# K's transform as 64 by 32 points in 32x64 tiles, the second table's magnitudes by 512 small exponentials, and a new order

## The chip, the cores and the metric

One core of one Trainium2 chip. TensorE (PE) multiplies matrices; its weight loads are a row of their own in the profile (PEld). VectorE (DVE) and ScalarE (ACT) do elementwise work, ScalarE also the exponentials, sines and sigmoids. SyncE (SP) issues every DMA. The metric is device microseconds of the core, as the median of several runs; the profile is one execution, and its span begins at its first and ends at its last record.

## The reference, cut to what matters

```
x = A_u[0]                                  # 2048 x 512
dt = exp(log_dt)                            # 512
P[d,n,l] = exp(dt[d]*(A_re + 1j*A_im)[d,n] * l)          # 512 x 128 x 2048
K[d,l] = real(sum_n C[d,n] * P[d,n,l] * dt[d]*B[d,n])    # 512 x 2048
a = causal_convolution(x, K) + x*Dskip      # by FFT of length 4096
b = (sigmoid(x @ w_gate) * (x @ w_up)) @ w_down          # 512 -> 1792 -> 512
g = sigmoid(sum(x*gate_w))
out = g*a + (1-g)*b
```

Everything is float32.

## The kernel before, in words

**Two strands.** The gated product `b` is the larger part of PE's work: `hidden` (line 894, tile `gups`) and `down` (line 946, tile `dps`), each product as three float32r matmuls of split halves. 2016 such matmuls of 512 columns run in all; they are called f matmuls here. A `gups` pair (gate and up) takes 12 matmuls each; ScalarE's sigmoid (line 911) releases the gate's bank, VectorE's product (line 913) the up's, ScalarE and VectorE then make the two halves `h` (lines 917, 918), which `dps` needs.

**The convolution.** The filter K is made in 16 groups of 32 channels. For one group, `bases` makes the tile `ex` (sines and cosines of 38 angles, lines 385 to 401) and `ep` (line 387 and the exponential of line 402), then the tile `bz` (lines 407, 409). `tables` makes two tables: `T` by a start (lines 439 to 442) and five doublings (lines 422 to 424), and `B`, 64 complex powers, whose magnitudes are an outer product of 8 by 8 exponentials on VectorE (line 451, twice a group) and which four VectorE products (lines 456 to 460) then turn by the angles. `ex` has one buffer, which those four products free. PE joins T and B (`kps`, line 476), ScalarE copies the result to `kst` (line 490), `first` transforms it (`wps`, line 503), ScalarE writes it to `kev` (line 515), and it goes to memory as `a_k`. x's first stage (`ups`, line 556) goes to `a_u`.

**The passes.** After the first 8 groups for one half of the channels, and after all 16 for the other, eight passes each do: second stage of x (`s2u`, line 639), second stage of K (`s2k`, line 664, twice a pass, each with its own weights `wwk` from memory), the products of the two (lines 673 to 680 on VectorE), the inverse (`ips`, line 700), and at the end `finals` (`fps`, line 748).

**Buffers.** PSUM has 8 banks: 3 for `gups`, 1 for `dps`, 4 (called XB) for everything of the convolution.

**What sets the order.** `Plan` takes the next instruction of any strand whose start would come first by a table of costs written in the code, plus a weight for each strand (`BIAS`), and so lays down one fixed order for each engine's queue. At run time each engine works its queue in that order and waits where a result isn't there. Plan's costs decide where something stands, not how long it takes.

Of the kernel before, what the change touches and what calls it, by code (L numbers as in the profile page):

```python
# [31 lines left out]
P = 128  # L32
# [5 lines left out]
NQ = 4  # L38
# [3 lines left out]
POWERS = list(range(0, 64, 8)) + list(range(8)) + ANGLES[33:]  # L42
# [8 lines left out]
BIAS = dict(ustep=0.15, inv=0.29, x=-4.3, w=-6.82, split=0.39, rows=-0.24, dn=0.48, urest=1.97, bases=0.29, tables=0.29,  # L51
            first=0.19, hidden=0.81, post=0.21, down=0.68, add=0.14, passes=0.06, step=0.35, finals=0.62, last=0.45, const=2.37,
            steps=-4.83, preludes=0.34, pw=-2.74)
CHANGE = dict(ACT=0.77, PE=2.53)

XLATE = 0
PACE = [4.21, 15.45]
SLACK = dict(dma=0.23, eng=0.04)
EARLY = -0.06
# [3 lines left out]
def constants():  # L63
    l1, k1 = np.arange(32)[:, None], np.arange(32)[None, :]
    ph = 2 * np.pi * l1 * (k1 + 0.25) / 32
    fwd = np.stack([np.cos(ph), -np.sin(ph)])
    wk = np.zeros((2, 2, 32, 2, 2, 32))
    for j in range(2):
        for c in range(2):
            wk[:, j, :, c, j, :] = fwd[c]  # L70
# [7 lines left out]
    wf = fwd.reshape(P, 64) / L  # L78
    l2, k2 = np.arange(32)[:, None], np.arange(32)[None, :]
# [10 lines left out]
    l2, k2 = np.arange(64)[:, None], np.concatenate([np.arange(0, 64, 2), np.arange(1, 64, 2)])[None, :]  # L90
    wwk = np.zeros((32, 2, 64, 2, 64))
    for k in range(32):
        th = 2 * np.pi * (l2 * (k + 0.25 + 32 * k2) % L) / L
        co, si = np.cos(th), np.sin(th)
        wwk[k, 0, :, 0], wwk[k, 0, :, 1], wwk[k, 1, :, 0], wwk[k, 1, :, 1] = co, -si, si, co
    f = lambda x, *s: np.ascontiguousarray(x.astype(np.float32).reshape(s))
    return {
        "c_wu": f(wu, P, P), "c_wf": f(wf, P, 64), "c_wk": f(wk, P, 2, 64),
        "c_pw": f(np.concatenate([ANGLES, POWERS]), 1, NA + NP),
        "c_wwu": f(wwu, 8, P, 2 * P), "c_wwv": f(wwv, 8, P, 2 * P),  # L100
        "c_wwk": f(wwk.reshape(16, 2, P, P).transpose(0, 2, 1, 3), 16, P, 2 * P),
# [133 lines left out]
def body(ctx, tc, xp, xt, prm, ldt, dsk, gw, wgu, wdn, c_wu, c_wf, c_wk, c_wwu, c_wwv, c_wwk, c_pw, out):  # L235
# [12 lines left out]
    a_k = [dr.tile([w // 64, P, 32, 64], F32, name=f"a_k{j}") for j, w in enumerate(WIDTHS)]  # L248
# [19 lines left out]
    wk = cst.tile([P, 2, 64], F32, name="wk")  # L268
# [14 lines left out]
    def steps():  # L283
        st = erl.tile([16, 10, 32], F32, name="steps")
        x, nf, r, e, h1, h2 = (st[:, i] for i in range(6))
        n, pn, b1, b2 = (st[:, i].bitcast(I32) for i in range(6, 10))
# [16 lines left out]
        def scale():  # L303
            for s in (0.5, 1.0):
                V.tensor_scalar(pn, nf, s, None, op0=OP.mult)
                h, b = (h1, b1) if s < 1 else (h2, b2)
                V.tensor_copy(h, pn)
                if s == 1.0:
                    V.tensor_tensor(h, h, h1, op=OP.subtract)
                V.tensor_scalar(b, h, 127.0, 8388608.0, op0=OP.add, op1=OP.mult)  # L310
                V.tensor_tensor(e, e, b.bitcast(F32), op=OP.mult)
# [9 lines left out]
        ("pg", 1, [P, 6, QW]), ("pp", 1, [P, 2, 2, QW]), ("bz", 1, [P, 3, 5, 32]), ("ex", 1, [P, 32, 2, NA]), ("ep", 1, [P, 32, NP]),  # L321
        ("ta", 1, [P, 32, 2, 32]), ("tb", 1, [P, 32, 2, 64]), ("t2", 2, [P, 32 * NA]), ("kst", 1, [P, 8, 64]), ("kev", 1, [P, 32, 64])))
# [5 lines left out]
    def preludes():  # L328

        yield E["dt"]  # L330
        for k in range(NG // NQ):
# [30 lines left out]
            left[pps] = 2 * NQ  # L362
# [9 lines left out]
    def bases():  # L372

        yield E["pw"]
        for gi in range(NG):
# [8 lines left out]
            sh, sa = [P, 32, NP], [P, 32, NA]  # L384
            t = yield "DVE", dve(32 * NA), lambda: V.tensor_tensor(  # L385
                f, pp[:, 0, 1, d, None].to_broadcast(sa), pw[:, None, :NA].to_broadcast(sa), op=OP.mult), t0 + [exs.t]
            te = yield "DVE", dve(32 * NP), lambda: V.tensor_tensor(
                ep, pp[:, 0, 0, d, None].to_broadcast(sh), pw[:, None, NA:].to_broadcast(sh), op=OP.mult), t0 + [eps.t]
# [13 lines left out]
            te = yield "ACT", ("exp", act(32 * NP)), lambda: A.activation(ep, ep, AF.Exp), [te]  # L402
# [5 lines left out]
                bz[:, 0::2], trig, ep[:, :, 16:].rearrange("p d k -> p k d")[:, None].to_broadcast([P, 2, 5, 32]), op=OP.mult), [t, te, bzs.t]  # L408
            ti = yield "ACT", 0.23, lambda: A.activation(bz[:, 1], bz[:, 2], AF.Copy, scale=-1.0), [t]
            base[gi][1] = bz, pp[:, 1, :, d], pps, ex, ep, bzs, exs, eps  # L410
# [16 lines left out]

    def tables():
        for gi in range(NG):
            j = max(i for i in range(NW) if OFF[i] <= 32 * gi)  # L430
            yield base[gi][0]
            bz, w, pps, ex, ep, bzs, exs, eps = base[gi][1]
# [12 lines left out]
            tbs, = yield TB, 1  # L445
            B = tbs.tile("B")
            tb = max(base[gi][0].t, tbs.t)

            sh = [P, 16, 8, 8]
            for d in (slice(0, 16), slice(16, 32)):  # L450
                tm = yield "DVE", dve(1024), lambda: V.tensor_tensor(  # L451
                    B[:, d, 0].rearrange("p d (a b) -> p d a b", b=8), ep[:, d, 0:8, None].to_broadcast(sh),
                    ep[:, d, None, 8:16].to_broadcast(sh), op=OP.mult), [tb]
            eps.free(tm)
            hi, lo = ex[:, :, :, :32], ex[:, :, :, 32:0:-1]
            yield "DVE", dve(1024), lambda: V.tensor_tensor(B[:, :, 1, 32:], B[:, :, 0, 32:], hi[:, :, 1], op=OP.mult), [tb]
            yield "DVE", dve(1024) + 0.1, lambda: V.scalar_tensor_tensor(
                B[:, :, 1, :32], B[:, :, 0, :32], -1.0, lo[:, :, 1], op0=OP.mult, op1=OP.mult), [tb]
# [167 lines left out]
    def ustep(j, wus, wwu, s2, au, ready, ta):  # L626
# [16 lines left out]
        for s in s2:  # L643
            s.free(t)
# [40 lines left out]
    def inverse(j, p, wvs, wwv, ready, both, tv):  # L685
# [18 lines left out]
        for s in ufs:  # L704
            s.free(t)
# [338 lines left out]
```

## Time and profile before

| | us |
|---|---|
| median of 3 runs | 649.28 (648.16 to 650.12) |
| the profiled execution | 648.06 |
| its span | 646.3 |

The page gives, for each engine, its busy time, its share of the span and its instructions; the groups, the timeline and the windows are other views of the same execution. In a timeline row the first number is the start and the second the time from the first start to the last end of the merged instructions, so the distance of two starts tells what a block takes from its engine; the second number alone overlaps the next row.

### The profile page before, as it was taken

To read this page: it belongs to the slowest core of one execution; us is meant where nothing else is said; L and a number is where in the kernel's file an instruction comes from. 1 tells how busy PE (TensorE), PEld (TensorE's weight loads), DVE (VectorE), ACT (ScalarE), POOL (GpSimd) and SP (SyncE) were. 2 spreads that over 40 slices of the span, in tenths; PEclk is the share of its full clock that TensorE was granted. 3 is DMA by queue.
4 is the path that set the end of the run, shared out by engine and by line. 5 is a ranking of instruction groups with operands and counts; after the bars stand their busy time and mean duration, and the time that the engine had idled before them with its cause. 6 is when DMAs were issued, how large, how long until landed. Compare 5 with 4: busy or idle time off the path is not lost.

```text
span 646.3 us, 15757 instructions
## 1 busy us (share of the span) xinstructions
PE 631.1 (98%) x6560; PEld 468.3 (72%) x6560; DVE 555.8 (86%) x953; ACT 374.3 (58%) x584; POOL 0.2 (0%) x4
## 2 busy tenths in 40 slices
PE   4999999999999999999999999999999999999996
PEld 3777777777787778877766787867787776666664
DVE  6859999999999999999999999999999836546515
ACT  5788787857677666576566857564676221333210
POOL 0000000000000000000000000000000000000000
PEclk9999999999999999999999999999999999999999
DMA  7974763745574446569158674542195688798377
GB/s 225 385 243 176 235 195 102 285 143 199 200 294 131 180 164 227 178 236 349 29 186 261 222 263 150 177 132 74 38 337 185 213 268 261 203 301 244 86 247 265
DMA packets 79622, 133.93 MB, mean 207 GB/s; under 512 B 7104, under 2 KB 53056, under 8 KB 74944
## 3 DMA queue, kind: packets, MB, share of 16 engines
q1 hardware_dynamic: 79552, 132.94, 62.5%
q8 instruction: 51, 0.84, 0.5%
q14 instruction: 19, 0.16, 0.1%
HBM read 79.43 MB, written 53.48 MB: 206 GB/s over the span
## 4 chain that ended last, share of the span: by engine, by line
PE 78%; DVE 14%; ACT 3%; issue 2%; DMA 1%; DVEq 0%; SPq 0%
PE gups L894 39%; PE dps L946 20%; PE kps L476 5%; PE s2k L664 4%; PE wps L503 2%; PE ips L700 2%; PE ups L556 2%; PE s2u L639 2%; PE fps L748 2%; DVE T L424 1%; DVE T L423 1%; DVE ex L395 1%; DVE t L422 1%; DVE sg L913 1%; DVE acc L966 1%
## 5 line engine op out<-in xcount | busy, mean ns | idle before, releaser
L894 PE MATMUL gups<-x,gu 128*128 128x512 f32 x1344 | 329.9, 395 | 9.2 <-ACT x L815 6.4
L894 PEld LDWEIGHTS gups<-x,gu 128*128 128x128 f32 x1344 | 251.6, 189 | 74.7 <-issue 10.0
L946 PE MATMUL dps<-dnw,h 128*128 128x512 f32 x672 | 177.5, 400 | 0.5 <-DVE h L918 0.2
L946 PEld LDWEIGHTS dps<-dnw,h 128*128 128x128 f32 x672 | 121.6, 188 | 42.7 <-issue 12.0
L917 ACT ACTIVATE h<-sg 128x512 fp32r<-128x512 f32 x56 | 35.1, 628 | 76.6 <-DVE sg L913 76.3
L673 DVE TENSOR_TENSOR tt<-s2k,uf 128x512 f32<-128x512 f32 x32 | 22.0, 688 | 31.7 <-PE s2k L664 30.7
L913 DVE TENSOR_TENSOR sg<-gups,sg 128x512 f32<-128x512 f32 x56 | 38.4, 686 | 11.5 <-PE gups L894 6.1
L515 ACT ACTIVATE kev<-wps 128x256 f32<-128x256 f32 x64 | 33.1, 672 | 25.3 <-PE wps L503 25.3
L422 DVE TENSOR_TENSOR t<-T,bz 128x64 f32<-128x64 f32 (+4 forms) x80 | 46.0, 575 | 1.0
L424 DVE TENSOR_TENSOR T<-T,t 128x64 f32<-128x64 f32 (+4 forms) x80 | 46.2, 577 | 0.7
L423 DVE TENSOR_TENSOR T<-T,bz 128x64 f32<-128x64 f32 (+4 forms) x80 | 46.0, 575 | 0.0
L966 DVE SCALAR_TENSOR_TENSOR acc<-dps,omg,acc 128x512 f32<-128x512 f32 x48 | 35.8, 747 | 10.4 <-PE dps L946 10.2
L918 DVE TENSOR_TENSOR h<-sg,h 128x512 fp32r<-128x512 f32 x56 | 38.5, 687 | 5.1 <-ACT h L917 4.9
L709 ACT ACTIVATE ev<-ips 128x256 f32<-128x256 f32 x64 | 19.8, 388 | 35.6 <-PE ips L700 32.8
L911 ACT ACTIVATE sg<-gups 128x512 f32<-128x512 f32 x56 | 33.5, 599 | 8.1 <-PE gups L894 7.9
L451 DVE TENSOR_TENSOR B<-ep 128x1024 f32<-128x1024 f32 x32 | 37.9, 1218 | 0.0
L476 PEld LDWEIGHTS kps<-B,T 128*32 128x32 f32 x2048 | 29.6, 110 | 6.8 <-issue 4.0
L394 ACT ACTIVATE af<-ex 128x1216 int32<-128x1216 f32 x16 | 19.6, 1222 | 25.3 <-DVE ex L385 25.3
L476 PE MATMUL kps<-B,T 128*32 128x64 f32 x2048 | 32.2, 220 | 0.6 <-DVE T L424 0.2
L664 PE MATMUL s2k<-ak,wwk 128*64 128x256 f32 x256 | 31.4, 386 | 0.0
L911 ACT ACT_TABLE_LOAD x23 | 29.5, 1283 | 0.4
L398 ACT ACTIVATE af<-ex 128x1216 f32<-128x1216 f32 x16 | 19.6, 1225 | 17.3 <-DVE ex L395 17.3
(79 smaller groups left out, 657.7 us busy)
## 6 DMA issues: line engine op xcount, KB each, us to landing
wsp<-gu SPq DMA_DIRECT2D x14, 1024.0 KB, 4.8
gu<-wsp SPq DMA_DIRECT2D x14, 1024.0 KB, 5.2
a_u<-evu SPq DMA_DIRECT2D x32, 256.0 KB, 3.7
a_k<-kev SPq DMA_DIRECT2D x8, 1024.0 KB, 4.8
au<-a_u SPq DMA_DIRECT2D x32, 256.0 KB, 4.4
ak<-a_k SPq DMA_DIRECT2D x32, 256.0 KB, 4.4
b_s<-ev SPq DMA_DIRECT2D x32, 256.0 KB, 4.2
b_in<-b_s SPq DMA_DIRECT2D x32, 256.0 KB, 3.5
```

The costliest lines, as they stand in the source:

```text
L422: yield "DVE", dve(n), lambda: V.tensor_tensor(t2, src, sb, op=OP.mult), [t, slot.t]
L423: t = yield "DVE", dve(n), lambda: V.tensor_tensor(dst, src, br, op=OP.mult), [t]
L424: t = yield "DVE", dve(n), lambda: V.tensor_tensor(dst, dst, t2[:, :, ::-1], op=OP.add), [t]
L451: tm = yield "DVE", dve(1024), lambda: V.tensor_tensor(B[:, d, 0].rearrange("p d (a b) -> p d a b", b=8), ep[:, d, 0:8, None].to_broadcast ...
L476: mm(p[32 * jj:32 * jj + 32, s], T[:, ch, c], B[:, ch, c], start=(c == 0), stop=(c == 1), tile_position=(0, 32 * jj), skip_group_check=True)
L664: mm(p2[64 * kb_:64 * kb_ + 64, c], wwk[:, kb_, 64 * c:64 * c + 64], ak[:, :, kb_], start=True, stop=True, tile_position=(0, 64 * kb_), sk ...
L894: mm(p, gu[:, a, k, dc], x[:, b, dc], start=(dc + n == 0), stop=(dc == NC - 1 and n == 2))
L911: t = yield "ACT", ("sig", act(512)), lambda: A.activation(sg, pg_, AF.Sigmoid), [tg, ss.t]
L913: t = yield "DVE", dve(512), lambda: V.tensor_tensor(sg, pu, sg, op=OP.mult), [t, tu]
L918: t = yield "DVE", dve(512), lambda: V.tensor_tensor(h[:, 1], sg, h[:, 0].bitcast(F32), op=OP.subtract), [t]
L946: mm(p, h[:, a, 128 * s:128 * s + 128], dn[:, b], start=(f == f0 and n == 0), stop=(f == f0 + gn - 1 and n == 2))
L966: te = yield "DVE", dve(512) + 0.06, lambda: V.scalar_tensor_tensor(accs[t], p, omg[:, t:t + 1], accs[t], op0=OP.mult, op1=OP.add), [tp, b ...
```

## The change

K's first stage becomes 64 points (before 32) in 32x64 tiles with 128 columns of weights' product each, the halves of a row accumulated in PSUM; it takes four XB banks at once (before two), and `kev` and `a_k` change their order. K's second stage then has 32 points and uses x's own weights `wwu`; the 32 loads of `wwk` go, `s2k` is one step for a pass, with two XB banks, in the tile form of `s2u`. The loads of `ak` stay 32 of 256 KB, in pieces of 256 bytes (before 512). `big` is two buffers of double size, `uf` one of double size; `wwu` is held until `s2k` is done. The channels are permuted on the way in.

The outer product of magnitudes (line 451) goes, and `ep` shrinks from 672 to 160 columns. In its place the new strand `magnitudes` runs 32 exponentials a group on ScalarE, one for each channel, of 64 columns, with the channel's rate as a scale read from memory for each partition. The planner enters 16 of them with the cost `16 * 0.1`.

All of `BIAS`, `CHANGE`, `PACE` and `EARLY` are new, so the order of every queue is another.

```diff
-BIAS = dict(ustep=0.15, inv=0.29, x=-4.3, w=-6.82, split=0.39, rows=-0.24, dn=0.48, urest=1.97, bases=0.29, tables=0.29,
+BIAS = dict(ustep=-0.13, inv=-0.0, x=-1.84, w=-0.87, split=0.5, rows=0.21, dn=-0.72, urest=0.59, bases=0.18, tables=0.37,
...
-POWERS = list(range(0, 64, 8)) + list(range(8)) + ANGLES[33:]
+POWERS = list(range(64)) + ANGLES[33:]
...
-            te = yield "DVE", dve(32 * NP), lambda: V.tensor_tensor(
-                ep, pp[:, 0, 0, d, None].to_broadcast(sh), pw[:, None, NA:].to_broadcast(sh), op=OP.mult), t0 + [eps.t]
+            te = yield "DVE", dve(160), lambda: V.tensor_tensor(
+                ep, pp[:, 0, 0, d, None].to_broadcast(sh), pw[:, None, NA + 64:].to_broadcast(sh), op=OP.mult), t0 + [eps.t]
...
-            te = yield "ACT", ("exp", act(32 * NP)), lambda: A.activation(ep, ep, AF.Exp), [te]
+            te = yield "ACT", ("exp", act(160)), lambda: A.activation(ep, ep, AF.Exp), [te]
...
+    def magnitudes(gi, second):
+        _, _, re, pps, ex, _, exs = base[gi][1]
+        tbs, = yield TB, 1
+        B = tbs.tile("B")
+        tb = max(base[gi][0].t, tbs.t)
+        for d in (0, 16):
+            def exps():
+                for ch in range(d, d + 16):
+                    A.activation(B[:, ch, 0], pw[:, NA:NA + 64], AF.Exp, scale=re[:, ch:ch + 1])
+            te = yield "ACT", ("exp", 16 * 0.1), exps, [tb]
+        used(pps, te)
+        hi, lo = ex[:, :, :, :32], ex[:, :, :, 32:0:-1]
+        yield "DVE", dve(1024), lambda: V.tensor_tensor(B[:, :, 1, 32:], B[:, :, 0, 32:], hi[:, :, 1], op=OP.mult), [te]
...
+        exs.free(tb)
+        second[1] = B, tbs
+        second[0].set(tb)
...
-            sh = [P, 16, 8, 8]
-            for d in (slice(0, 16), slice(16, 32)):
-                tm = yield "DVE", dve(1024), lambda: V.tensor_tensor(
-                    B[:, d, 0].rearrange("p d (a b) -> p d a b", b=8), ep[:, d, 0:8, None].to_broadcast(sh),
-                    ep[:, d, None, 8:16].to_broadcast(sh), op=OP.mult), [tb]
...
-        banks = yield XB, 2
-        ph = [b.tile("wps") for b in banks]
+        banks = yield XB, 4
+        ph = [b.tile("wps", [P, 2, P]) for b in banks]
 
         def mms():
-            for s in range(8):
-                for jh in range(2):
-                    r = slice(64 * jh, 64 * jh + 64)
-                    for c in range(2):
-                        mm(ph[jh][64 * c:64 * c + 64, 64 * s:64 * s + 64], kst[r, s], wk[r, c], start=True, stop=True,
-                           tile_position=(64 * jh, 64 * c), skip_group_check=True)
+            for s in range(2):
+                for h in range(2):
+                    for x in range(0, 4, 2):
+                        for jj in range(4):
+                            r = slice(32 * jj, 32 * jj + 32)
+                            mm(ph[jj][32 * x:32 * x + 64, s], kst[r, h, 4 * s + x:4 * s + x + 2], wk[r, h],
+                               start=(h == 0), stop=(h == 1), tile_position=(32 * jj, 32 * x), skip_group_check=True)
...
-                    wks, = yield fin["wwk"], 1
-                    wwk = wks.tile("wwk")
-                    tw = yield "SP", kb(128), lambda: S.dma_start(wwk, c_wwk[q].rearrange("p (a b) -> p a b", a=2)), [wks.t]
...
         def mms():
             for c in range(2):
-                for kb_ in range(2):
-                    mm(p2[64 * kb_:64 * kb_ + 64, c], wwk[:, kb_, 64 * c:64 * c + 64], ak[:, :, kb_], start=True, stop=True,
-                       tile_position=(0, 64 * kb_), skip_group_check=True)
-        t = yield "PE", ("128x64", 3.45e-3 * w, 16.4), mms, [tk, bank.t]
+                for g_ in range(4):
+                    for r in range(2):
+                        rows_ = slice(64 * r, 64 * r + 64)
+                        mm(pk[r][32 * g_:32 * g_ + 32, c], wwu[rows_, g_, c], ak[rows_, :, g_], start=True, stop=True,
+                           tile_position=(64 * r, 32 * g_), skip_group_check=True)
+        t = yield "PE", ("64x32", 3.6e-3 * w, 65), mms, [tk] + [b.t for b in banks]
```

**What it does to the queues, at three places.** Counted over the whole program, ScalarE's table loads go from 58 to 69 (the exponentials of line 424 of the changed kernel have 5, the sigmoids 4 and 2 more), PE's blocks of f matmuls from 86 to 95, and the direct neighbourhoods of two blocks of other kinds from 21 to 13. The 16 `kps` stand behind 225 to 1689 f matmuls before, and behind 219 to 1608 now.

The first place is ScalarE's queue around the second group's `kst`, which the third group's magnitudes follow. Before, from `bz` on (`sg` is a sigmoid, `acc` the first sum of `dps`, `h` and `dnw` halves of a split):

```order
L409 ACTIVATE bz_987<-bz_987 128x160
L490 ACTIVATE kst_1064<-kps_997 128x512
L546 ACT_TABLE_LOAD
L546 ACTIVATE g_87<-gl_89 128x1
L547 ACTIVATE omg_88<-gl_89 128x1
L911 ACTIVATE sg_1086<-gups_960 128x512
L962 ACTIVATE acc_1090<-dps_894,omg_88 128x512
```

And now:

```order
L487 ACTIVATE kst_1170<-kps_1064 128x8x2x32
L424 ACT_TABLE_LOAD
L424 ACTIVATE B_1183<-pw_86,pp_220 128x64 x32
L902 ACT_TABLE_LOAD
L902 ACTIVATE sg_1260<-gups_1072 128x512
L806 ACTIVATE gu_1075<-st_1076 128x512
L806 ACTIVATE gu_1075<-st_1078 128x512
L563 ACTIVATE evu_1096<-ups_1083 128x512
L563 ACTIVATE evu_1096<-ups_1084 128x512
L908 ACTIVATE h_1296<-sg_1260 128x512
```

The 32 exponentials now stand ahead of the sigmoid of `gups_1072`, with a table load on each side of them.

PE's queue at the same place, now:

```order
L473 MATMUL kps_1064<-B_790,T_766 32x64 x64
L937 MATMUL dps_1062<-dnw_1033,h_979 128x512 x3
L885 MATMUL gups_1072<-x_94,gu_569 128x512 x12
L885 MATMUL gups_1224<-x_94,gu_569 128x512 x12
L885 MATMUL gups_1259<-x_111,gu_569 128x512 x12
L885 MATMUL gups_1278<-x_111,gu_569 128x512 x6
```

`gups_1278` is the third `gups` tile behind `gups_1072` and there are three banks, so it takes the bank that the sigmoid of `gups_1072` releases.

The second place is ScalarE's queue at the tenth group's `kst`, with the eleventh group's magnitudes (`ev` is the eviction of the inverse, `uf` that of `s2u`):

```order
L487 ACTIVATE kst_4212<-kps_4127 128x8x2x32
L424 ACTIVATE B_4230<-pw_86,pp_3001 128x64 x32
L701 ACTIVATE ev_4297<-ips_4258 128x256
L701 ACTIVATE ev_4297<-ips_4259 128x256
L701 ACTIVATE ev_4297<-ips_4260 128x256
L701 ACTIVATE ev_4297<-ips_4261 128x256
L953 ACTIVATE acc_4224<-dps_3927,omg_88 128x512
L637 ACTIVATE uf_4298<-s2u_4309 128x512
```

Here the evictions that give the four XB banks back stand behind the exponentials. On PE, between that `kps` and the next `wps`, stand 3 `dps`, 6 `gups`, the inverse, 6 `gups`, `s2u`, and 9 `dps`.

The third place is one pass near the end on PE. Before:

```order
L700 MATMUL ips<-uf,wwv 64x256 x16
L946 MATMUL dps<-dnw,h 128x512 x3
L639 MATMUL s2u<-au,wwu 32x256 x16
L664 MATMUL s2k<-ak,wwk 64x256 x8
L894 MATMUL gups<-x,gu 128x512 x18
```

And now:

```order
L693 MATMUL ips<-uf,wwv 64x256 x16
L885 MATMUL gups<-x,gu 128x512 x6
L632 MATMUL s2u<-au,wwu 32x256 x16
L655 MATMUL s2k<-ak,wwu 32x256 x16
L885 MATMUL gups<-x,gu 128x512 x18
```

`s2k` keeps its place behind `s2u`, in 16 matmuls of the same form as those in place of 8 of another.

201 lines of the change are left out of this document (92 added, 109 removed).

## The prediction

> **What bounds the kernel now.** First the page's busy shares and the chain that ended last, then two windows, one over the stage in which the groups of K are made and one over what follows.
>
> ```profile
> span 646.3 us, 15757 instructions
> PE 631.1 (98%) x6560; PEld 468.3 (72%) x6560; DVE 555.8 (86%) x953; ACT 374.3 (58%) x584; POOL 0.2 (0%) x4
> ...
> PE 78%; DVE 14%; ACT 3%; issue 2%; DMA 1%; DVEq 0%; SPq 0%
> ...
> 60.00:480.00 420.00, 418.75 (x4773) 319.29 (x4772) 410.94 (x681) 284.57 (x427) 0.00 (x0) 1.00 0.58 192
> 480.00:646.30 166.30, 160.91 (x1586) 110.61 (x1584) 99.33 (x177) 47.06 (x91) 0.00 (x0) 1.00 0.75 232
> ```
>
> In the windows the columns after the length are PE, PEld, DVE and ACT. PE is the bound: from 60 to 480 us it lacks 1.25 us of being busy throughout. VectorE stands right beside it in that stage (411 of 420 us), ScalarE has 135 us free there (68% busy). After 480 us only PE is full. So time is won by less PE work, as long as neither VectorE nor ScalarE comes late to what PE waits for; and in the first stage neither is far from it.
>
> **The change: PE.** The second view is PE's timeline, read by distances of starts, at two places.
>
> ```profile
> 243.59 2.88 PE L946 MATMUL dps<-dnw,h 128*128 128x512 f32 x12
> 246.31 1.52 PE L894 MATMUL gups<-x,gu 128*128 128x512 f32 x6
> ...
> 253.99 1.16 PE L503 MATMUL wps<-wk,kst 64*64 64x64 f32 x64
> 255.08 1.66 PE L894 MATMUL gups<-x,gu 128*128 128x512 f32 x6
> ...
> 588.67 1.09 PE L639 MATMUL s2u<-au,wwu 64*32 64x256 f32 x32
> 589.69 1.95 PE L664 MATMUL s2k<-ak,wwk 128*64 128x256 f32 x16
> 591.57 4.37 PE L894 MATMUL gups<-x,gu 128*128 128x512 f32 x18
> 595.87 1.12 PE L700 MATMUL ips<-uf,wwv 32*64 32x256 f32 x32
> 596.92 1.66 PE L894 MATMUL gups<-x,gu 128*128 128x512 f32 x6
> ```
>
> An f matmul takes 2.72/12 = 0.227 us; a block of them behind another kind costs 4.30 - 18 x 0.227 = 0.22 us beyond its matmuls. `s2k` takes 1.88 us a pass, `s2u` 1.02. The new `s2k` has exactly `s2u`'s form and count, so 16 x 0.86 = 13.8 us go. Nine more f blocks give back 9 x 0.22 = 2.0 us. `wps` takes 1.09 now; its new form is that of `ips` (1.05), with as many columns in all, so 0 to 0.6 us, taken as 0.3 of gain; four banks at once cost nothing on PE by themselves, since the order already places them. PE's sum is 12.1 us less.
>
> **VectorE.** The rows of the groups that go or shrink, and two of the timeline:
>
> ```profile
> L451 DVE TENSOR_TENSOR B<-ep 128x1024 f32<-128x1024 f32 x32 | 37.9, 1218 | 0.0
> L387 DVE TENSOR_TENSOR ep<-pp,pw 128x672 f32<-128x672 f32 x16 | 13.6, 852 | 0.0
> ...
> 195.76 1.23 DVE L456 TENSOR_TENSOR B<-B,ex 128x1024 f32<-128x1024 f32 x1
> 196.90 1.22 DVE L457 SCALAR_TENSOR_TENSOR B<-B,ex 128x1024 f32<-128x1024 f32 x1
> ...
> 200.31 0.27 DVE L422 TENSOR_TENSOR t<-T,bz 128x64 f32<-128x64 f32 x1
> 200.49 0.27 DVE L423 TENSOR_TENSOR T<-T,bz 128x64 f32<-128x64 f32 x1
> ```
>
> 37.9 us go, and `ep` with 160 columns lies between its own 0.85 and the 0.27 of 64 columns, by columns near 0.36: another 8 us. This is worth nothing by itself, for PE sets the end. Its worth is room: about 2.9 us a group.
>
> **ScalarE.** The exponential over `ep` shrinks and 512 small ones come.
>
> ```profile
> L402 ACT ACTIVATE ep<-ep 128x672 f32<-128x672 f32 x16 | 12.3, 767 | 0.2
> L409 ACT ACTIVATE bz<-bz 128x160 f32<-128x160 f32 x16 | 5.4, 336 | 16.7 <-DVE bz L407 16.5
> L911 ACT ACT_TABLE_LOAD x23 | 29.5, 1283 | 0.4
> ...
> 52.88 0.20 ACT L546 ACTIVATE g<-gl 128x1 f32<-128x1 f32 x1 [1.67 <-DVE ju L541]
> 52.99 0.19 ACT L547 ACTIVATE omg<-gl 128x1 f32<-128x1 f32 x1
> 53.08 1.21 ACT L394 ACTIVATE af<-ex 128x1216 int32<-128x1216 f32 x1
> 54.19 0.67 ACT L962 ACTIVATE acc<-dps,omg 128x512 f32<-128x512 f32 x1
> 54.76 0.62 ACT L917 ACTIVATE h<-sg 128x512 fp32r<-128x512 f32 x1
> ...
> 71.18 0.59 ACT L911 ACTIVATE sg<-gups 128x512 f32<-128x512 f32 x1
> 71.66 1.58 ACT L567 ACTIVATE evu<-ups 128x512 f32<-128x512 f32 x3
> ```
>
> One column takes 0.19 us and the next instruction starts 0.10 to 0.11 us after it, so neighbours overlap by about 0.1. 160 columns take 0.34: 64 take some 0.25 by the line between. The new ones read their scale from memory for each partition; the only row of that kind shown is line 962, which takes 0.67 against 0.59 for the sigmoid of the same size, 0.08 more, and starts no later and hands over no earlier (0.57 us from start to start, against 0.48). So 0.25 + 0.08 = 0.33 us each, 0.23 apart. The bounds are 0.10 apart (one column, no scale) and 0.33 (no overlap). I take 0.23, since every step of it has a row: 32 x 0.23 = 7.4 us a group.
>
> [...]
>
> By the load's row 11 more cost 14 us of ScalarE. In the 60 to 480 us stage 14 groups are made (28 of the 32 instructions of line 451):
>
> ```profile
> 60.00:480.00 420.00, 33.20 (x28) 1.00 0.58 192
> ```
>
> ScalarE's 285 us there become 285 + 14 x (7.4 - 0.4) + 13 = 396 of 420, 94%. Three engines would then be near full in queues of fixed order.
>
> **Where it reaches PE.** The order leaves 32 x 0.1 = 3.2 us for a group's exponentials; 7.4 means 4.2 us more at each. I walk PE and ScalarE through places of the order, clock zero at the end of `kps`, with the distances above (`kst` done at 0.7, a sigmoid 0.6, a 512 column copy 0.5, a 1024 column product on VectorE 1.14).
>
> First place (third group): table load to 2.0, exponentials to 5.2 with the order's room or 9.4 with mine, load and sigmoid to 7.1 or 11.3. PE does 3 `dps` and three `gups` tiles by 9.1 and then needs that sigmoid's bank: no wait, or 2.2. The next `wps` needs four XB banks, and the last of them comes from `evu` copies behind the sigmoid; then `dps` needs an `h` whose product stands on VectorE behind the four products of B, which end at 9.8 or 14.0. With those PE is 3.7 us late in all.
>
> Second place (eleventh group): exponentials to 3.9 or 8.1, then the evictions of the inverse. PE has done 3 `dps`, 6 `gups`, the inverse and 6 `gups` by 4.9 and needs two XB banks for `s2u`: at 4.9 or at 8.9. 4.0 us late.
>
> The ninth group has 18 more `dps` around its `wps`; there PE comes to wait only for the VectorE sum behind B's products (14.6 against 13.1): 1.5 late. At the twelfth group the sigmoid's bank is needed at 9.5 and comes at 12.4: 2.9. The mean of the four is 3.0 us. All queues are late by the same amount behind such a place, so nothing is caught up. Four groups (the first, fourth, fifth and fifteenth) have over 13 us of matmuls ahead of the first one that would wait; I count 12: 36 us, and between 12 x 1.5 = 18 and 12 x 4.0 = 48.
>
> **DMA.**
>
> ```profile
> au<-a_u SPq DMA_DIRECT2D x32, 256.0 KB, 4.4
> ak<-a_k SPq DMA_DIRECT2D x32, 256.0 KB, 4.4
> ...
> wwk<-c_wwk SPq DMA_DIRECT2D x32, 128.0 KB, 4.0
> wwu<-c_wwu SPq DMA_DIRECT2D x16, 128.0 KB, 4.3
> ```
>
> `ak`'s pieces halve to 256 bytes, at the same 32 issues; `au` with larger pieces lands after the same 4.4 us, so I take nothing, up to 1 us a pass in the last eight if it bound (8 us), against 32 loads of `wwk` that go. `wwu` is freed by `s2k`, 1 us later than by `s2u`; the next is needed some 9 us on and lands in 4.3.
>
> **The sum.** 646.3 - 12.1 + 36 = 670.2 us of span. The profiled execution took 648.06, 1.8 more than its span, and the median is 1.2 above that: 673 us. With 18 or 48 for the waits 655 or 685.
>
> **Rivals.**
> The exponentials come 0.10 to 0.12 us apart, as the order has them. For: neighbours of one column do. Against: 64 columns and the scale each have a row that adds. Then PE's sum alone counts: 634.2 + 3.0 = 637 us, faster. It decides below the point where the waits equal the 12.1 us: a place passes on 3.0 of 4.2, so 1.2 are absorbed; 12.1/12 = 1.0 passed on is 2.2 more than the room, 5.4 us for 32, 0.17 us apart.
>
> They cost 0.23, but the room that VectorE gained takes up most, and only waits for a sigmoid's bank stay, at six or seven groups with about 2 us each: 634.2 + 13 + 3 = 650, no change. Against: at two of four places the wait went through other banks.
>
> They don't overlap: 0.33 apart, 10.6 us a group, 3.2 more than I take, passed on in full: 673 + 12 x 3.2 = 711.
>
> **Chances.** The forecast 0.63, the fast exponentials 0.18, the absorbed waits 0.14, no overlap 0.05. The forecast's own range is 655 to 688; taking in the absorbed case and half of the fast one it is 637 to 690. What a measurement of this kernel can tell from no change is about 0.3%, 2 us. Faster by more: 0.18 and a third of the absorbed case, 0.22; within: 0.05; slower: 0.73.
>
> **What would show it.** Right: 32 instructions of line 424 with starts 0.23 us apart; ScalarE above 90% in the stage of the groups; PE idle there for 20 to 45 us, ended by sigmoids, `ev` or `evu` copies and VectorE products that follow B's; `s2k` blocks of 1.0 us. Wrong: starts 0.10 apart with PE full; or PE's waits ended by DMAs, or lying behind 500 us; or `s2k` still near 1.9.

## The result and the profile after

| | before | after |
|---|---|---|
| median, us | 649.7 (648.16 to 652.94) | 723.08 (722.54 to 725.4) |
| the profiled execution | 648.06 | 725.4 |
| its span | 646.3 | 723.2 |
| mean granted clock of PE | 1.00 | 0.955 |

After over before is 1.1129, with a 95% interval of 1.108 to 1.1178: 11% slower. The median lies 50 us above the forecast of 673, 38 above the 685 that the upper bound of the waits gave, and 33 above 690, the end of the stated range; the direction came as forecast, the size did not.

First the page of the changed kernel: busy times, the clock in 40 slices, the chain, and the two groups in which the change shows.

```profile
span 723.2 us, 16678 instructions
PE 651.2 (90%) x6816; PEld 476.5 (66%) x6816; DVE 519.4 (72%) x928; ACT 496.7 (69%) x1100; POOL 0.2 (0%) x4
...
PEclk9998999989899999999899999988999999999999
...
PE 60%; ACT 24%; DVE 8%; DMA 5%; issue 2%; SPq 1%; ACTq 0%; DVEq 0%
...
L424 ACT ACTIVATE B<-pw,pp 128x64 f32<-128x64 f32 x512 | 124.0, 334 | 0.1
...
L428 DVE TENSOR_TENSOR B<-B,ex 128x1024 f32<-128x1024 f32 x16 | 19.6, 1225 | 73.9 <-ACT B L424 73.9
```

ScalarE has gone from 3% of the chain that ended last to 24%, VectorE from 14% to 8%. VectorE now stands idle for 73.9 us in front of line 428, the first product behind the exponentials: 4.6 us in each of 16 groups. PE is not busy for 723.2 - 651.2 = 72.0 us; before it was 15.2.

The windows of the two stages (after the length: PE, PEld, DVE, ACT, POOL, then PE's granted clock):

```profile
60.00:480.00 420.00, 379.61 (x4265) 279.84 (x4265) 335.52 (x592) 349.02 (x782) 0.00 (x0) 0.94 0.56 172
480.00:723.20 243.20, 226.57 (x2389) 162.79 (x2388) 146.17 (x252) 104.38 (x234) 0.00 (x0) 0.99 0.64 182
```

From 60 to 480 us no engine is full: PE works 380 of 420 us, VectorE 336, ScalarE 349. That is how three queues of fixed order look when each waits for the other in turn. The view of PE's waits has these rows among others, such as those of the start (us in all, how often, the longest):

```profile
PE dps L937 <- DVE acc L957: 12.7, 4, 4.3
PE gups L885 <- ACT sg L902: 11.2, 4, 3.9
PE s2u L632 <- ACT ev L701: 11.0, 3, 4.2
...
PE fps L740 <- ACT kev L511: 4.4, 1, 4.4
PE dps L937 <- ACT acc L953: 4.2, 1, 4.2
PE ups L552 <- ACT kev L511: 3.4, 1, 3.4
PE kps L473 <- DVE T L412: 3.1, 1, 3.1
PE wps L501 <- ACT evu L563: 2.5, 1, 2.5
```

4 + 4 + 3 + 1 + 1 + 1 + 1 + 1 = 16 waits, 52.5 us together, and in PE's timeline each of the 16 blocks of exponentials has one of them behind it. Several kinds of releaser take their turn, by what the order has put behind the exponentials at each place. The third group, which the prediction walked through first, in the timelines of PE, ScalarE and VectorE:

```profile
126.08 2.93 PE L885 MATMUL gups<-x,gu 128*128 128x512 f32 x6 [2.64 <-ACT sg L902]
128.94 1.22 PE L501 MATMUL wps<-wk,kst 32*64 32x128 f32 x64
...
115.06 1.28 ACT L424 ACT_TABLE_LOAD   x1
116.35 7.77 ACT L424 ACTIVATE B<-pw,pp 128x64 f32<-128x64 f32 x32
124.14 1.28 ACT L902 ACT_TABLE_LOAD   x1
125.43 0.60 ACT L902 ACTIVATE sg<-gups 128x512 f32<-128x512 f32 x1
...
124.16 1.22 DVE L428 TENSOR_TENSOR B<-B,ex 128x1024 f32<-128x1024 f32 x1 [5.11 <-ACT B L424]
```

32 exponentials take 7.77 us, (7.77 - 0.334)/31 = 0.24 apart. The sigmoid stands behind them and a table load, PE's next `gups` behind the sigmoid: 2.64 us, where the prediction had 2.2.

The six f matmuls behind that wait then take 2.86 us to the start of `wps`; at the 0.227 us of before they would take 1.36. The windows from that place on show why:

```profile
116.00:120.00 4.00, 4.00 (x19) 3.31 (x18) 2.87 (x8) 3.99 (x17) 0.00 (x0) 1.00 1.01 381
...
124.00:128.00 4.00, 1.92 (x5) 1.53 (x6) 3.85 (x4) 3.97 (x7) 0.00 (x0) 0.70 0.00 0
128.00:132.00 4.00, 4.00 (x75) 2.88 (x74) 4.00 (x6) 2.52 (x5) 0.00 (x0) 0.87 0.63 156
132.00:136.00 4.00, 4.00 (x17) 2.48 (x17) 4.00 (x8) 3.79 (x9) 0.00 (x0) 1.00 0.50 176
```

The granted clock is 1.00 up to the wait, 0.70 and 0.87 in the two windows behind it, and 1.00 again. So a wait costs more than its length, and the prediction had no term for that.

### The profile page after: what moved, and what is told of

The parts are those of the page before. It is cut to its first block, busy times and chain, and to the rows that moved or that the text cites. A ratio compares the mean times of both kernels' runs of the same rounds, so it can differ in the third digit from the quotient of the medians.

```text
span 723.2 us, 16678 instructions
## 1 busy us (share of the span) xinstructions
PE 651.2 (90%) x6816; PEld 476.5 (66%) x6816; DVE 519.4 (72%) x928; ACT 496.7 (69%) x1100; POOL 0.2 (0%) x4
## 4 chain that ended last, share of the span: by engine, by line
PE 60%; ACT 24%; DVE 8%; DMA 5%; issue 2%; SPq 1%; ACTq 0%; DVEq 0%
PE gups L885 29%; PE dps L937 17%; ACT B L424 17%; PE kps L473 4%; PE s2u L632 2%; PE s2k L655 2%; DMA ak<-a_k 2%; PE fps L740 2%; PE ups L552 2%; PE ips L693 2%; DMA st<-xt 2%; DVE B L428 1%; PE wps L501 1%; DVE B L432 1%; DVE B L429 1%
## 5 line engine op out<-in xcount | busy, mean ns | idle before, releaser
L885 PE MATMUL gups<-x,gu 128*128 128x512 f32 x1344 | 342.6, 406 | 22.0 <-ACT sg L902 11.2
L885 PEld LDWEIGHTS gups<-x,gu 128*128 128x128 f32 x1344 | 258.4, 195 | 95.4 <-issue 15.3
L937 PE MATMUL dps<-dnw,h 128*128 128x512 f32 x672 | 186.4, 418 | 18.6 <-DVE acc L957 12.7
L937 PEld LDWEIGHTS dps<-dnw,h 128*128 128x128 f32 x672 | 127.2, 197 | 69.1 <-DVE acc L957 16.0
L424 ACT ACTIVATE B<-pw,pp 128x64 f32<-128x64 f32 x512 | 124.0, 334 | 0.1
L428 DVE TENSOR_TENSOR B<-B,ex 128x1024 f32<-128x1024 f32 x16 | 19.6, 1225 | 73.9 <-ACT B L424 73.9
L902 ACT ACTIVATE sg<-gups 128x512 f32<-128x512 f32 x56 | 33.7, 601 | 15.3 <-PE gups L885 15.0
L511 ACT ACTIVATE kev<-wps 128x256 f32<-128x256 f32 x64 | 32.3, 648 | 12.2 <-PE wps L501 12.1
L632 PE MATMUL s2u<-au,wwu 64*32 64x256 f32 x512 | 21.6, 425 | 11.2 <-ACT ev L701 11.0
```

What stands on the lines that cost most here:

```text
L424: A.activation(B[:, ch, 0], pw[:, NA:NA + 64], AF.Exp, scale=re[:, ch:ch + 1])
L632: mm(pu[r][32 * g_:32 * g_ + 32, c], wwu[rows_, g_, c], au[rows_, g_], start=True, stop=True, tile_position=(64 * r, 32 * g_), skip_group_ ...
L885: mm(p, gu[:, a, k, dc], x[:, b, dc], start=(dc + n == 0), stop=(dc == NC - 1 and n == 2))
L902: t = yield "ACT", ("sig", act(512)), lambda: A.activation(sg, pg_, AF.Sigmoid), [tg, ss.t]
L937: mm(p, h[:, a, 128 * s:128 * s + 128], dn[:, b], start=(f == f0 and n == 0), stop=(f == f0 + gn - 1 and n == 2))
```

## The experiments

The runs that follow use the changed kernel's line numbers, except where their own edits shift them. Their ratios are against runs of the kernel before on the same chip.

**The exponentials alone, with the order as it is.** Four kernels keep the instruction order of all queues and change only how long a group's magnitudes hold ScalarE. In them channels share a rate or take a constant, so they compute another K and serve for the time alone. The first takes four channels in one instruction:

```diff
-                for ch in range(d, d + 16):
-                    A.activation(B[:, ch, 0], pw[:, NA:NA + 64], AF.Exp, scale=re[:, ch:ch + 1])
+                for ch in range(d, d + 16, 4):
+                    A.activation(B[:, ch:ch + 4, 0], pw[:, None, NA:NA + 64].to_broadcast([P, 4, 64]), AF.Exp, scale=re[:, ch:ch + 1])
```

> The changed kernel with its order untouched; only the 32 exponentials of a group become 8 of 256 columns (four channels share the first one's rate, so K is another). By the changed kernel's rows (0.333 us for 64 columns, 0.24 from start to start) one of 256 should take 0.50 and follow the next 0.40 later, 3.2 us a group, which is what the order left room for. Theory A (the exponentials' length alone makes the loss, by waits in queues of fixed order and by the slower clock behind them): VectorE's wait for them falls from 74 us to under 10, the mean clock is 0.99 or more, and the time is 637 to 645 us. Rival B (the new order, the four XB banks of the first stage or the smaller pieces of ak make it): 700 us or more. Rival C (a part each): 660 to 695 us.

Measured: 640.13 us, ratio 0.985 (0.982 to 0.9881). From its page and its view of VectorE's waits:

```profile
span 636.5 us, 16294 instructions
PE 618.9 (97%) x6816; PEld 458.5 (72%) x6816; DVE 518.4 (81%) x928; ACT 426.6 (67%) x716; POOL 0.2 (0%) x4
...
DVE B L428 <- ACT B L424: 5.5, 11, 0.8
```

The changed transform, the table loads and the whole new order are still in it; only the 7.7 us a group became 3.2 to 3.3, what the order has room for. PE works 618.9 us in place of the 631.1 of before: 12.2 less, where the sum had 12.1. With this order, all of the loss hangs on the length of the exponentials.

The second takes two channels at a time, the third one at a time with a constant in place of the scale from memory:

```diff
-                for ch in range(d, d + 16):
-                    A.activation(B[:, ch, 0], pw[:, NA:NA + 64], AF.Exp, scale=re[:, ch:ch + 1])
+                for ch in range(d, d + 16, 2):
+                    A.activation(B[:, ch:ch + 2, 0], pw[:, None, NA:NA + 64].to_broadcast([P, 2, 64]), AF.Exp, scale=re[:, ch:ch + 1])
```

```diff
-                    A.activation(B[:, ch, 0], pw[:, NA:NA + 64], AF.Exp, scale=re[:, ch:ch + 1])
+                    A.activation(B[:, ch, 0], pw[:, NA:NA + 64], AF.Exp, scale=-0.05)
```

> As the one before, but 16 exponentials of 128 columns a group (two channels share a rate): 0.39 us each, 0.29 apart, 4.7 us a group, 1.5 over the room. Theory A with the steps of the prediction (a place absorbs about 1.2 us, the rest is passed on): 640 to 650 us. Theory A with nothing absorbed, as the 74 us of VectorE's wait in the changed kernel suggest (4.6 us at each of 16 groups): 16 x 1.5 = 24 us of waits and some of the clock, 660 to 675 us. Rival B: 700 us or more.

> The changed kernel with its order untouched; the 32 exponentials of 64 columns take a constant scale instead of one read from memory for each partition (all magnitudes alike, so K is another). This prices that operand: 0.25 us each and 0.15 apart if it costs what line 962 suggests, 4.7 us a group, and then the same time as the run with 16 of 128 columns within 1%. If the operand costs more than its own 0.09 us (it disturbs neighbours), clearly faster than that run; if it costs nothing, 0.33 and 0.24 stay and the time stays at 723.

Measured: 658.41 and 658.32 us, one execution each. The group of the exponentials and VectorE's wait for them, of the one and of the other:

```profile
L424 ACT ACTIVATE B<-pw,pp 128x128 f32<-128x128 f32 x256 | 76.8, 391 | 0.1
...
DVE B L428 <- ACT B L424: 27.0, 15, 2.3
```

```profile
L424 ACT ACTIVATE B<-pw 128x64 f32<-128x64 f32 x512 | 76.6, 244 | 0.1
...
DVE B L428 <- ACT B L424: 26.7, 15, 2.3
```

Two quite different ways to spend some 4.7 us of ScalarE a group give the same time to 0.1 us (their spans, 656.3 and 655.5, differ by 0.8): it is the length that counts, not the form. The scale from memory costs 334 - 244 = 90 ns an instruction, near the 0.08 of the prediction. And 1.5 us over the room cost 19.8 us of span (656.3 against 636.5). Of these 11.9 are time in which PE isn't busy, 0.74 us at each of 16 places, where a place that absorbs 1.2 us would have passed on 0.3.

The fourth stands between these and the change, half of the channels in pairs and half alone:

```diff
-                for ch in range(d, d + 16):
+                for ch in range(d, d + 8, 2):
+                    A.activation(B[:, ch:ch + 2, 0], pw[:, None, NA:NA + 64].to_broadcast([P, 2, 64]), AF.Exp, scale=re[:, ch:ch + 1])
+                for ch in range(d + 8, d + 16):
```

> The changed kernel with its order untouched; of a group's exponentials 16 stay single and the other 16 become 8 of 128 columns (pairs share a rate, so K is another): 16 x 0.24 + 8 x 0.29 = 6.2 us a group, 3.0 over the order's room. The runs with 3.2 and 4.7 us gave spans of 636.5 and 656.3, 13.2 us for each us over the room, at a clock of 1.0. If the rest of the changed kernel's loss is the same waits and the clock falls only behind waits longer than some 3 us: span 676, clock 0.99 or more. If the clock falls with any wait: 685 to 695 and a clock of 0.97 to 0.98. By the straight line the changed kernel (4.5 us over) would have 696; it has 723, so the clock would be worth 27 us there.

Measured: 689.8 us, one execution; span 687.5, mean clock 0.984, PE busy 637.0. The span is that of the forecast in which the clock falls with any wait; the clock lies between the two. VectorE's wait for the exponentials:

```profile
DVE B L430 <- ACT B L426: 50.4, 16, 3.8
```

With that the same order has been run with four lengths of the same work:

| us a group | span | PE busy | PE not busy | VectorE's wait | mean clock |
|---|---|---|---|---|---|
| 3.2 | 636.5 | 618.9 | 17.6 | 5.5 | 1.000 |
| 4.7 | 656.3 | 626.8 | 29.5 | 27.0 | 1.000 |
| 6.2 | 687.5 | 637.0 | 50.5 | 50.4 | 0.984 |
| 7.7 (the change) | 723.2 | 651.2 | 72.0 | 73.9 | 0.955 |

PE's idle time grows by 7.9 us for each us in the first step and by 14 in the two others: nearly all of what 16 groups are late by (16 us for each), with some taken up only at the start. PE's busy time grows too, for the same matmuls in the same order: by 7.9 us at 4.7 us a group, where the clock is still full and the reason stays open, and by 24.4 more up to the change, where the clock falls.

**The transform alone.** The outer product on VectorE is put back (as in the kernel before), the transform stays changed, first with the change's merge weights, then with weights found for these costs. The core of the edit:

```diff
-        for d in (0, 16):
-            def exps():
-                for ch in range(d, d + 16):
-                    A.activation(B[:, ch, 0], pw[:, NA:NA + 64], AF.Exp, scale=re[:, ch:ch + 1])
-            te = yield "ACT", ("exp", 16 * 0.1), exps, [tb]
+        sh = [P, 16, 8, 8]
+        for d in (slice(0, 16), slice(16, 32)):
+            te = yield "DVE", dve(1024), lambda: V.tensor_tensor(
+                B[:, d, 0].rearrange("p d (a b) -> p d a b", b=8), ep[:, d, 0:8, None].to_broadcast(sh),
+                ep[:, d, None, 8:16].to_broadcast(sh), op=OP.mult), [tb]
```

> The changed kernel's transform and weights, but the magnitudes by the outer product of 8 by 8 exponentials on VectorE as in the kernel before (ep with 672 columns again), the order made anew by the planner with the changed kernel's weights. Theory A: without the 512 exponentials PE's sum decides, 12 us under before: 634 to 642 us, faster than before by 1 to 2%. Rival (VectorE, at 98% in the stage of the groups, is the next bound, or the weights don't suit): 648 to 665 us. Rival B: 690 us or more.

Measured: 746.3 us, ratio 1.1486 (1.1467 to 1.1505), a miss: slower than the change itself. Its page shows where:

```profile
PE   5988999999999999999999999999999846666543
...
PEclk9998999999999999999999999999999975666555
```

PE is full for three quarters of the span and then starves: the last nine slices of 18.6 us are 3 to 8 tenths busy. The f work, which fills PE's time between the steps of the convolution, has run out by then, because weights that were chosen for magnitudes on ScalarE let the convolution fall behind when VectorE makes them. So this run says something of the weights and nothing of the transform. With weights of its own, here without those of `BIAS`:

```diff
-CHANGE = dict(ACT=0.2, PE=1.65)
-PACE = [17.46, 8.71]
-EARLY = 3.05
+CHANGE = dict(ACT=0.65, PE=1.45)
+PACE = [1.4, 7.3]
+EARLY = 20.75
```

> The changed transform with all magnitudes by the outer product on VectorE, as before the change, and merge weights found for these costs in place of those of the change. The whole of K is computed. Beside the run of 746 us with the change's weights this tells the transform from the weights. If the weights made those 746 us: 632 to 655 us; the lower end if PE alone sets the end (646.3 - 12.1 + 3 = 637), the upper if VectorE, which has no relief here (555.8 us busy before), comes to be waited for. If the transform itself hinders (four XB banks at once for the first stage, smaller pieces of ak): 665 us or more, with PE's waits ended by XB evictions or by ak.

Measured: 663.95 us, ratio 1.0214 (1.0193 to 1.0236), between the two forecasts. The weights were 82 of the 96 us that the first run lay above the kernel before. For the rest, the chain that ended last, the window of the groups and a row of PE's waits:

```profile
DVE 40%; PE 39%; DMA 10%; issue 5%; ACT 4%; SPq 2%; DVEq 0%; ACTq 0%
...
60.00:480.00 420.00, 407.85 (x4823) 305.16 (x4822) 402.65 (x669) 272.06 (x414) 0.00 (x0) 1.00 0.60 188
...
PE s2u L629 <- ACT ev L698: 6.9, 14, 0.5
```

VectorE is on 40% of the chain (14% before the change), at 403 of 420 us: the chain points at VectorE, which gets no relief, as what keeps the 12 us of PE's work from the span. That isn't shown by a run of its own. The sign of the other forecast came in part: of PE's 35.5 us of not being busy, 6.9 are waits for evictions that free XB banks and 1.9 are for `ak`. The run at 3.2 us a group has the same transform and 0.7 us of such waits in all, so the transform does not force them. Whether another order would do without them here is open.

**The cost that the planner enters.** The measured 0.24 in place of 0.1, first with the change's weights, then with weights found for it:

```diff
-            te = yield "ACT", ("exp", 16 * 0.1), exps, [tb]
+            te = yield "ACT", ("exp", 16 * 0.24), exps, [tb]
```

> The changed kernel, with one number of the planner corrected: 16 exponentials are entered as 16 * 0.24 and not 16 * 0.1, the weights as they are; so the order is another and the work the same. Theory A (the order was laid for exponentials three times too fast): VectorE's wait for line 428 falls below 20 us and the clock rises over 0.98. What the time does depends on whether ScalarE has room for 7.7 us a group at all: with room, 640 to 665 us; if ScalarE (about 94% full in the stage by the prediction's count) is then the bound, the stage of the groups is stretched instead and it stays between 680 and 725 us.

> The changed kernel with all 512 exponentials, their measured cost entered (16 x 0.24 for half a group) and merge weights found for these costs. The whole of K is computed. Against the run with the same number and the change's weights (715 us). If the wrong number and the weights that were found for it are the cause: 640 to 665 us, the granted clock 0.98 or more; ScalarE then works about 500 of 650 us and the order can place that. If 7.7 us of exponentials a group do not fit on ScalarE in any order: 680 us or more, with PE's longest waits ended by ScalarE as they are in the changed kernel.

Measured: 715.29 us (one execution), and 682.66, ratio 1.0501 (1.0468 to 1.0534). VectorE's wait for the exponentials and some of PE's waits, of the first and of the second:

```profile
DVE B L428 <- ACT B L424: 5.0, 10, 0.9
...
PE gups L885 <- ACT sg L902: 16.1, 10, 5.2
```

```profile
DVE B L426 <- ACT B L422: 4.7, 9, 0.9
...
PE ups L550 <- DMA u<-xp: 13.3, 1, 13.3
PE gups L883 <- ACT sg L900: 7.7, 4, 2.9
```

The right number does what it should to the wait that it is about (73.9 to 5.0 and to 4.7 us), and yet both kernels are slow. In the first PE waits for sigmoids instead, its last slices are 4, 5 and 3 tenths busy, and the mean clock is 0.948, where over 0.98 was expected. Its time lies in the range for ScalarE as the bound, but ScalarE is busy 359 of 420 us in the stage of the groups, so it isn't full. The second stays 5% slower than before, with other holes in the span, a wait of 13.3 us for a load at the very start among them. Its time agrees with the forecast that 7.7 us a group don't fit, though the sign (PE's longest waits ended by ScalarE) came only in part. It isn't shown that no order could hold them.

**The outer product on GpSimd**, with the changed transform and weights found for it; against the outer product on VectorE above, the edit is

```diff
-            te = yield "DVE", dve(1024), lambda: V.tensor_tensor(
+            te = yield "POOL", 2.4, lambda: nc.gpsimd.tensor_tensor(
```

> The changed kernel's transform, with the outer product of magnitudes on GpSimd, which has nothing else to do, entered as 2.4 us each; new weights. No row so far prices a GpSimd product of 1024 columns. If it takes 2.4 us or less and doesn't slow VectorE: 640 to 652 us. If it takes 4 us or more, or VectorE's 1024 column products grow over their 1.22 us beside it: 660 us or more.

Measured: 707.47 us, ratio 1.0883 (1.0773 to 1.0992). The groups of GpSimd's product and of two small products of VectorE that grew, and behind them the same two in the kernel before:

```profile
L420 POOL TENSOR_TENSOR B<-ep 128x1024 f32<-128x1024 f32 x32 | 67.5, 2128 | 470.5 <-PE kps L470 379.8 <-ACT ep L387 38.9 <-PE wps L498 27.3
...
L446 DVE TENSOR_TENSOR pp<-pp,ex 128x64 f32<-128x64 f32 x16 | 28.2, 1765 | 0.6
L445 DVE TENSOR_TENSOR T<-pp,ex 128x64 f32<-128x64 f32 x16 | 17.3, 1084 | 7.9 <-PE kps L470 7.9
```

```profile
L439 DVE TENSOR_TENSOR T<-pp,ex 128x64 f32<-128x64 f32 x16 | 4.4, 276 | 1.8 <-PE kps L476 1.7
L440 DVE TENSOR_TENSOR pp<-pp,ex 128x64 f32<-128x64 f32 x16 | 4.4, 276 | 0.6
```

The two products of 64 columns take 1084 and 1765 ns on average in place of 276, and the one of 32 columns behind them (line 447) 1070 in place of 217; the four of 1024 columns that turn B, which need GpSimd's result and so run behind it, take 1216 and 1217 (1218 to 1223 before). The slow ones stand where GpSimd's start: in 13 of the 16 groups its first product waits for `kps`, and line 445 waits for `kps` too, 8 times. In three groups in GpSimd's timeline its two take 4.08, 4.69 and 4.09 us together. So what was to be taken off VectorE comes back as busy time: 577.1 us, above the 555.8 of before. That GpSimd's products make them longer is read from these rows; no run shows it alone. How much of the 707 us comes from this and how much from the order was not told apart.

**Half and half.** 16 of a group's channels by exponentials, 16 by the outer product on VectorE, once with the measured cost and weights found for it, once with the order of the change kept as it is. The second, where the product stands ahead of line 428's (`eo` are the 16 exponentials of a channel whose outer product is taken):

```diff
-                for ch in range(d, d + 16):
+                for ch in range(16 + d // 2, 24 + d // 2):
...
+        def outer():
+            V.tensor_tensor(B[:, :16, 0].rearrange("p d (a b) -> p d a b", b=8), eo[:, :, 0:8, None].to_broadcast(sq),
+                            eo[:, :, None, 8:16].to_broadcast(sq), op=OP.mult)
+            V.tensor_tensor(B[:, :, 1, 32:], B[:, :, 0, 32:], hi[:, :, 1], op=OP.mult)
+        yield "DVE", dve(1024), outer, [te]
```

> The changed transform; of a group's 32 channels, 16 get their magnitudes by exponentials of 64 columns on ScalarE, entered with the measured cost (16 x 0.24 = 3.8 us), the other 16 by the outer product on VectorE as before the change (one product of 1.22 us a group), and the merge weights are new, for these costs. The whole of K is computed. Theory A (ScalarE was only mis-entered, and nothing else in the change costs time): PE's sum counts, 646.3 - 12.1 = 634.2 us of span and some 3 us around it, 634 to 642 us, the wait of VectorE for the magnitudes below 10 us in all and the granted clock 0.99 or more. Theory B (ScalarE beside the stage is too full for any share of the exponentials, whatever number is entered): 645 us or more, with PE's longest waits ended by ScalarE. Theory C (an order found for one set of costs only fits by luck, as in the run with the outer product): 660 us or more, with PE starved near the end.

> The changed kernel with its order kept as it is on every queue; in each group 16 of the 32 channels keep their exponentials on ScalarE (16 x 0.24 = 3.9 us, where the order leaves 3.2), the other 16 take an outer product of 1.22 us on VectorE, ahead of the product that follows the exponentials, with 256 columns more in the tile ep (some 0.2 us more on ScalarE and 0.3 on VectorE). The whole of K is computed. By the four runs with this order (636.5 us of span at 3.2 us a group, 656 at 4.7, 687.5 at 6.2, 723 at 7.7) 3.9 us alone make 636.5 + 0.7 x 13 = 646 of span. Theory A (the order's room is what counts, and VectorE's product runs while the exponentials do): 640 to 650 us, no slower than before the change, and the clock 0.99 or more. Theory B (VectorE, at 395 of 420 us in this stage when the exponentials fitted, has no room for 1.5 us more a group, and comes late with the products that follow): 655 to 672 us, with PE's waits ended by VectorE's sums (acc) and products (h).

Measured: 653.67 us, ratio 1.0051 (1.0025 to 1.0076), and 653.56, ratio 1.0052 (1.0033 to 1.0072). The first has the time of its theory B but not its sign (PE's waits for ScalarE are 8.4 us at the start and 3.5 in all behind it), the second lies between its two forecasts; both are 0.5% slower than the kernel before. The second's page:

```profile
PE 627.1 (96%) x6816; PEld 458.9 (70%) x6816; DVE 541.3 (83%) x960; ACT 438.4 (67%) x844; POOL 0.2 (0%) x4
...
L438 DVE TENSOR_TENSOR B<-B,ex 128x1024 f32<-128x1024 f32 x16 | 19.6, 1225 | 2.0 <-ACT B L429 0.6
```

With the order untouched, handing half of the exponentials back to VectorE takes away 69.5 of the 73.4 us that the change had lost, and VectorE's wait for them falls from 73.9 to 0.6. What is left over the 3.2 us run (15.3 us of span) is the 0.7 us over the room, by the table some 6 to 9 us, and VectorE's 23 us of more work (VectorE is on 33% of the chain, 5% in the 3.2 us run); the two were not told apart. No version that computes the whole of K came out ahead of the kernel before; the run at 640 us shows what the transform and the order would be worth with magnitudes that cost ScalarE 3.3 us a group and VectorE nothing.

## Why the prediction was wrong, point by point

**PE's work: right.** -12.1 us in the sum, -12.2 by busy time in the run with the order kept and the short exponentials. A pass of `s2k` shows its 1.02 us in the timeline of the changed kernel:

```profile
600.02 1.09 PE L655 MATMUL s2k<-ak,wwu 64*32 64x256 f32 x32
601.04 5.73 PE L885 MATMUL gups<-x,gu 128*128 128x512 f32 x24
```

`wps` gained nothing (1.14 us a block against 1.09), a miss of about 1 us in all.

**The exponentials: right.** 0.23 apart and 0.33 long were taken; 0.24 and 0.334 came. The terms came too: 244 ns without the scale from memory, where 0.25 us was taken, and 334 with it, 90 more where 0.08 us was taken; starts 0.24 us apart make an overlap of 0.09, where 0.10 was taken. 128 columns with the scale took 391 ns.

**Where they reach PE: the places were right, their count wrong.** The walk gave 2.2 us for the third group's wait for the sigmoid, 1.5 for the ninth's for the sum, 4.0 for the eleventh's for the evictions and 2.9 for the twelfth's for the sigmoid; PE's timeline has 2.64, 3.40, 3.05 and 2.80, each with the releaser that was named. The mean of the four measured ones is 3.0, as taken, but by luck: the third place was put at 3.7 in all and the ninth at 1.5, errors that cancel. What failed is the sentence that four groups (the first, fourth, fifth and fifteenth) have over 13 us of matmuls ahead of the first one that would wait, so that 12 count. All 16 wait: those four 4.18, 4.26, 3.42 and 1.87 us in PE's timeline, 13.7 together. From the end of `kps` PE comes to the matmul that waits after 10.1 us in the fourth group, 7.0 in the fifth and 11.8 in the fifteenth; in the first, where no `kps` stands ahead, it comes there 6.4 us behind the start of the exponentials. In the fourth it is a `dps`, and its releaser is VectorE's sum `acc`, which stands behind the late products of B. The term was 36, with 48 as its upper bound; it measured 52.5, 13.7 of it in the four places and 38.8 in the twelve.

**The 1.2 us that a place absorbs: wrong by the runs between.** It was to give the point of no loss at 5.4 us a group. At 4.7 us the kernel is slower than before already (658 against 650). The mean of the sixteen waits, 3.3 of the 4.5 us over the room, does leave 1.2 absorbed, but at 1.5 over only 0.76 were, so it is no fixed amount.

**The clock: missing, and the largest error.** The sum has no term for matmuls that take longer behind a wait. For the same matmuls in the same order PE is busy 651.2 us in place of 618.9, 32.3 more. The clock's share is 24 us if the growth at full clock (7.9) is taken off, and 29 by busy time and missing clock, 651.2 x (1 - 0.955); both are estimates, the second since the mean clock is one over the whole span.

**The sum, corrected.** The run at 3.2 us a group has 636.5 of span (the prediction's 634.2 and little else). PE's idle time rises from 17.6 to 72.0, 54.4 us; its work stretches by 32.3: 723.2. That is 53.0 us above the 670.2 of the sum: 2.3 are what the run at 3.2 us lies above the 634.2, 18.4 (54.4 - 36) are PE's idle time, mostly waits counted too few, and 32.3 are the same work taking PE longer, most of it by the clock.

**The signs.** The starts 0.24 us apart and the `s2k` blocks came. ScalarE above 90% in the stage of the groups did not: it is busy 349 of 420 us, 83%, because the stage stretched and the exponentials of 12 groups lie in the window, where 14 were counted. PE's idle time there, 40 us, lies within the 20 to 45, but only because four of the sixteen waits lie outside the window.

**The rivals.** The fast exponentials (637) fell by the 0.24 in the trace, though the run at 640 us shows that 637 was nearly the right price for its condition. The absorbed waits (650) fell by the sixteen waits, only four of which are for a sigmoid's bank. No overlap (711) fell by the 0.24; that its time lay nearest is chance.

**DMA: worth nothing, as taken.** `ak` in smaller pieces does land later, after 5.5 us in place of 4.4 (the page's list of DMA issues), but PE waits 1.0 us for it over the whole changed kernel.

## What to carry to other kernels

In queues of fixed order the number that the order was laid out with is a deadline: work that takes longer than it was entered with makes everything behind it late, and the length of a wait has to be counted at every place where such work stands, by following each queue behind it to the first thing PE needs, sums and products as well as buffers. Entering the right number afterwards took the wait away here and not the loss (715 and 683 us), so the length itself has to be made to fit. A second price hung on waits of PE here: in the 3 us behind twelve of the sixteen, which took 2.51 to 4.41 us, the clock was 0.50 to 0.79. And weights found for one set of costs need not suit another: a part undone under the old weights (746 us) was worse than the change.

## What the runs showed of the hardware

**The clock gave way behind short waits.** Of the sixteen waits in the changed kernel, twelve are followed by 3 us of a granted clock between 0.50 and 0.79; among them one of 2.51 us, while one of 3.08 isn't. In each pair of these windows the first is the wait, the second the work behind it:

```profile
153.87:158.13 4.26, 0.00 (x1) 0.00 (x0) 4.26 (x6) 4.25 (x11) 0.00 (x0) 0.79 0.23 47
158.13:162.00 3.87, 3.86 (x9) 3.09 (x10) 3.06 (x9) 1.44 (x5) 0.00 (x0) 0.50 0.92 275
304.83:307.91 3.08, 0.00 (x1) 0.03 (x1) 3.04 (x4) 3.05 (x4) 0.00 (x0) 1.00 0.48 194
307.91:312.00 4.09, 4.09 (x137) 3.63 (x138) 3.11 (x6) 4.07 (x6) 0.00 (x0) 1.00 0.53 142
```

In the run at 6.2 us a group even a wait of 1.90 us was followed by 0.73:

```profile
303.87:305.77 1.90, 0.00 (x2) 0.01 (x1) 1.90 (x4) 1.23 (x2) 0.00 (x0) 1.00 1.00 354
305.77:308.77 3.00, 3.00 (x10) 2.39 (x11) 3.00 (x6) 1.73 (x2) 0.00 (x0) 0.73 1.06 322
```

In the run at 4.7 us, whose waits behind the start are all at most 1.6 us, the mean clock stays 1.000. The length of a wait alone doesn't tell the two kinds apart: in the changed kernel the twelve with a lower clock behind them took 2.51 to 4.41 us, the four with 1.00 behind them 1.82 to 3.08, and the one of 1.90 in the other run is shorter than two of those four. Why 2.51 brought the clock down and 3.08 did not stays open.

**VectorE's small products took longer beside GpSimd's.** In the run with the outer product on GpSimd 276 ns became 1084 and 1765 on average in products of 64 columns (lines 445, 446), and 217 became 1070 in one of 32 (line 447), behind the same `kps` as GpSimd's products of 2128 ns each. The four of 1024 columns that run behind GpSimd's kept their 1.22 us.
